# Attention scores in bundles of four and three beside a feed-forward product, and four parts instead of six behind the last value product

## The chip, the cores and the metric

The kernel runs on one core of one Trainium2 chip. The metric is the device time of one execution in microseconds (us), as the median of several runs. A profiled execution is recorded beside them; its span runs from the first to the last instruction of the core, and its own device time is a little longer than its span.

## The reference

The program is attention without a softmax, followed by a normalised two-layer feed-forward block with a residual:

```
S, D = 448, 64                      # 8 batches, 12 heads
scores = q @ k.T / sqrt(D)
attn   = max(scores, 0) ** 2 / S
x      = (attn @ v)                 # heads side by side: (8, 448, 768)
xn     = (x - mean) / sqrt(var + 1e-6) * g_ln
out    = x + max(xn @ w_ch1, 0) @ w_ch2     # 768 -> 3072 -> 768
```

Inputs and output are float32; the kernel computes the products in bf16.

## The kernel before

The eight batches are worked on two at a time, as four pairs 0 to 3. A pair goes through attention, the first feed-forward product (768 to 3072, with ReLU) and the second one (3072 to 768, with the residual). The change lies in the stage that is run three times, once for each of the pairs 0, 1 and 2 in the loop `for pair in range(pairs - 1)`: there the second feed-forward product of one pair is interleaved on TensorE with the attention of the next. I call these stages 0, 1 and 2. Between them lie the stages of the first product (`ffn1_pair`, line 960 in the profile), which uses seven block products in place of eight (Strassen), with sums made on VectorE and GpSimd or fetched.

The interleaving is written out in program order, and each engine runs its instructions in that order (the kernel opens a manual schedule). Two lists are merged by `spread`:

- The main list holds the second product in **parts** (also called units). A part is three matmuls, 128 by 128 weights with 384 columns, so `K2 // PARTS * DH` = 1152 columns. Eight parts make one output tile, behind which VectorE adds the residual and SP stores it. In stages 0 and 1 these are lines 789 and 800; in stage 2 the second product is the Strassen form (lines 1136, 1175, 1193). Stage 0 has 96 parts, stage 1 has 76 and stage 2 has 92 in the main list.
- The side list holds attention. Six **groups** of four heads each (two batches, three groups a batch) have seven **slots** each: a slot is 64 keys against 448 queries for the four heads. I write s0 to s6 for a group's slots and P for its value product.

A slot (`scores`) is four matmuls of 64 by 64 by 448 on the four quadrants of TensorE (line 400) into one PSUM buffer `sc_ps`; ScalarE then applies ReLU out of PSUM into an `attn_sb` tile in SBUF (line 411); the tile is then squared, either by ScalarE (line 413, when `act` is set) or by VectorE (line 380, when `square_fresh` or `pending` comes by). The value product P (`values`) is 28 matmuls of 64 by 64 by 448, in seven steps of four (line 432), into a buffer `av_ps` of the same pool; VectorE scales it into `xT_sb` (line 438). The pool `ps_sc` has **three** buffers, handed out in turn, for slots, value products and the `mean_ps` of `fold_mean` (line 512) alike; the parts' accumulators come from another pool, of two buffers. A group's value product comes in the bundle in which the next group's scores begin.

Before, `attention` cuts the 42 slots into 14 bundles of three, whatever group they belong to, and puts P behind the first or second slot of a bundle, where that slot is number 1 or 2 of the next group. Three orders of a bundle result: three slots; slot, slot, P, slot; and slot, P, slot, slot. The last P stands alone. `spread` gives all 15 pieces the same share of the stage's columns (`period`). The third slot of a bundle is squared on ScalarE in stages 0 and 2, and in every third bundle in stage 1.

In front of the last P the hook "odd" puts one or two sums for the next stage on VectorE (lines 989 and 994). Behind the last P, the hook "start" puts two more there (`x_sum`, lines 905 and 906, read by the third and fifth product of the next stage), then come the last `few` = 6 parts, and then `stage["run"]` begins the next first product with PSUM buffers `m_ps` in the room that `ps_sc` had. In stage 0, `fold_beside` also hangs `fold_mean` (four short matmuls, a copy by ScalarE) and `fold_into` (VectorE, line 519) on numbered parts; `fold_mean` takes a `ps_sc` buffer.

Of the kernel before, what the change touches and what calls it, by code (L numbers as in the profile page):

```python
# [24 lines left out]
            done += 1  # L25


def spread(main, cost, side, costs, pending):

    period = (cost * len(main) + sum(costs)) / sum(c > 0 for c in costs)
    at, due, done, n, ago = 0, period - costs[0], 0, 0, 0
    for unit in main:
        unit()
        at += cost
        ago += 1
        if ago % 2:
            pending(1)
        if n < len(side) and at >= (due if costs[n] else done + 3 * cost):  # L40
            if costs[n]:
                pending()
            side[n]()
            if costs[n]:
                at += costs[n]
                due += period
                done = at
                ago = 0
            n += 1
    for unit in side[n:]:  # L50
        pending()
        unit()
    pending()
# [3 lines left out]
def kernel(  # L57
# [28 lines left out]
    B, H, S, D = q.shape  # L86
# [3 lines left out]
    J = S // HP  # L90
# [4 lines left out]
    K2 = d_ff // P  # L95
    S2 = 2 * S
    NT = S2 // P
    DH = d_model // 2
# [117 lines left out]
    for queue, name, lo, hi in ((nc.sync, "q", 0, FEW), (nc.scalar, "k", 0, FEW),  # L216
                                (nc.sync, "k", FEW, J), (nc.scalar, "q", FEW, J)):
        s = slice(lo * D, hi * D)
# [304 lines left out]
    def fold_beside(units):  # L523

        more = {4: [lambda: statistics(0, 0), lambda: roots(0, 0, 1)], 24: [lambda: odd_x_out(0, nc.sync)]}
        for o in range(0, K2, K1):
            more[30 + 2 * o] = [lambda o=o: odd_h_out(0, nc.sync, (o, o + K1))]
        for i, n in ((2, 0), (3, 2), (4, 26), (5, 47)):
            more.setdefault(n, []).append(lambda i=i: fold_mean(i))
        for o in range(4 * K1):  # L530
            more.setdefault(6 + o * 84 // 24, []).append(lambda o=o: fold_into(2 + o // K1, o % K1))

        def both(n, unit):
            unit()
            for f in more.get(n, ()):
                f()
        return [lambda n=n, unit=unit: both(n, unit) for n, unit in enumerate(units)]

    by_dma = 2
# [96 lines left out]
    def attention(bs, hooks):  # L636

        lo, hi = bs[0] * G, (bs[-1] + 1) * G
        seq = [(n, i) for n in range(lo, hi) for i in range(J)]

        def item(n, i, act):
            scores(n, (i,), FULL, act)
            ahead = 3 if n + 3 < LATE else 2
            if i == J - 1 and n + ahead < len(groups) and (ahead == 3 or n + 2 >= LATE) and n != LATE - 1:
                transposed(n + ahead)  # L650

        def product(n):
            values(n, FULL)
            if n + 4 <= LATE:
                load(n + 4, "v")
            elif n + 3 > LATE:
                if n == LATE - 1:
                    put_off.append((n + 3, "v"))
                else:
                    load(n + 3, "v")  # L660

        squares = {by_dma: (0, 1, 2), by_dma + 2: (0,), B - 2: (0, 1, 2)}.get(bs[0], ())

        def bundle(items, at, turn):
            for o, it in enumerate(items):
                item(*it, o == 2 and turn in squares)
                if o == at:
                    product(it[0] - 1)
        units, costs, due = [], [], [[]]
        for s in range(0, len(seq), 3):  # L670
            items = seq[s:s + 3]
            at = max((o for o, (n, i) in enumerate(items[:2]) if n > lo and i in (1, 2)), default=-1)
            units.append(lambda items=items, at=at, s=s: bundle(items, at, s // 3 % 3))
            n = items[at][0] - 1
            costs.append((len(items) + (J if at >= 0 else 0)) * S)
            due.append([hooks[n - lo]] if at >= 0 and n - lo in hooks else [])
            for f in due.pop(0):
                units.append(f)
                costs.append(0)
        units.append(lambda: product(hi - 1))  # L680
        costs.append(J * S)
        return units, costs, due[0]


    xtok, rstd, moments = {}, {}, {}
# [1 line left out]
    def tokens_part(pair, lo, hi, chunks):  # L687

        for c in chunks:
            nc.sync.dma_start_transpose(xt_room[:, c, lo:hi], xT[pair][:, c, lo * P:hi * P])  # L690
# [89 lines left out]
    PARTS = 8  # L780
# [531 lines left out]
    units, side = ffn1_units(0, BLK[0][0]), attention_block(0, BLK[0][1])  # L1312
    units, late = units[:-4], units[-4:]
# [13 lines left out]
    units = ffn1_units(0, BLK[0][1])  # L1327
# [10 lines left out]
    side = {}  # L1338
# [61 lines left out]
    for pair in range(pairs - 1):  # L1400
        last = pair == pairs - 2
        following = {}

        def hook(name):
            if not following:
                following.update(ffn1_pair(
                    pair + 1, keep=pair == 0, given=pair > 0, late=last,
                    between=(between_one, between_two, between_three)[pair]))
                if pair:
                    tokens_room(pair + 1)  # L1410
            following[name]()
            if (pair, name) in soon:
                tokens_part(pair + 1, *soon[pair, name])
        if last:
            mm = [ps_mm.tile([P, 512], fp32, tag="mm", name="o_ps") for _ in range(2)]
            zs = [x_room.rearrange("p b c s -> p (b c s)")[:, 3 * KH * P:3 * KH * P + 2 * DH].bitcast(fp32),
                  room0[:, 9:].rearrange("p c n -> p (c n)").bitcast(fp32)]
            h_sum_tiles()
            head, units, _ = strassen_units(pair, mm, lambda t: mm[::-1] if t % 2 else mm)
        else:  # L1420
            units = ffn2_units(pair)
            head, units = (units[:PARTS // 2], units[PARTS // 2:]) if pair else ([], units)
        if pair:
            for unit in head:
                unit()
            stage["close"]()
            if pair == 1:
                odd_h_out(pair, nc.sync, (8, KH), (8 + KH, K2))
            narrow.close()
            ps_sc = open_wide()  # L1430
        else:
            units = fold_beside(units)
        if pair == 1:
            w2_sum_tiles()
            units = beside_of(units, dict(zip((20, 36, 50), w2_sum_units("t6"))))
        beside, costs, left = attention(
            [2 * pair + 2, 2 * pair + 3], {G - 1: lambda: hook("even"), 2 * G - 2: lambda: hook("odd")})
        few = 3 * PARTS // 4
        spread(units[:-few], K2 // PARTS * DH, beside, costs, square_fresh)
        for f in left:  # L1440
            f()
        wide.close()
        hook("start")
        ps_m = open_narrow()
        for unit in units[-few:]:
            unit()
        store_now()
        stage = following
        if pair == 0:
# [49 lines left out]
```

## Time and profile before

Three runs took 512.58, 512.78 and 513.10 us. The profiled execution took 512.57 us.

| | us |
|---|---|
| median of the runs | 512.78 |
| profiled execution | 512.57 |
| its span | 510.6 |
| stage 0, attention beside the second product (99.70 to 166.94 of the span) | 67.2 |
| stage 1 (213.70 to 274.07; it begins with the end of a first product) | 60.4 |
| stage 2 (320.70 to 390.48; likewise) | 69.8 |
| the two first products between them (166.94 to 213.70, 274.07 to 320.70) | 46.8 and 46.6 |
| from 390.48 to the end | 120.1 |

A line of the timeline gives the start in us, the duration in us, the engine, the line of the kernel, the operation with output and input tiles, the count, and in brackets the idle time ahead of it and who ended it. Neighbouring instructions of one kind are merged into one line. The ends of matmuls are modelled, so that one line overlaps the start of the next; a stretch of TensorE is better read from start to start.

### The profile page before, as it was taken

The page shows a single profiled execution, that of the slowest core. Times are in us where ns is not written, and L with a number is a line of the kernel's source. Part 1 is how long each engine was busy: PE and PEld are TensorE (multiplying, and loading weights), DVE is VectorE, ACT ScalarE, POOL GpSimd, SP SyncE. Part 2 cuts the span into 40 slices and gives each one's busy share as a digit, 9 for nine tenths or more (in the row PEclk, how much of TensorE's full clock was granted, in tenths as well). Part 3 has the DMA queues.
Part 4 walks back from the last instruction along what each step waited for, and adds up shares of the span by engine and source line. Part 5 has one row for each costly group of instructions (what it writes and reads, how often), then busy time and mean ns, then how long its engine had stood idle before and what let it go on. Part 6 is the DMA issues. An engine that isn't in the chain of part 4 may idle for free.

```text
span 510.6 us, 11501 instructions
## 1 busy us (share of the span) xinstructions
PE 503.1 (99%) x4545; PEld 297.9 (58%) x4545; DVE 388.2 (76%) x747; ACT 315.3 (62%) x519; POOL 130.0 (25%) x180
## 2 busy tenths in 40 slices
PE   8999999999999999999999999999999999999996
PEld 6677778955555555555555555555555555566663
DVE  4875755697998988768878888578869688677663
ACT  5966776578887566667883666489884677300000
POOL 8335102011412486002111995011000231000000
PEclk9999999999999999999999999999999999999999
DMA  9999999999999975739993878349936943622222
GB/s 198 206 206 206 211 206 143 135 195 177 203 203 223 219 228 152 191 87 163 269 170 75 177 167 140 61 78 179 194 69 164 224 131 94 230 64 63 63 62 62
DMA packets 136743, 80.25 MB, mean 157 GB/s; under 512 B 92418, under 2 KB 132610, under 8 KB 136690
## 3 DMA queue, kind: packets, MB, share of 16 engines
q1 hardware_dynamic: 106402, 46.59, 43.9%
q0 software_dynamic: 28272, 29.92, 36.7%
q10 hardware_dynamic: 2016, 3.02, 2.4%
q8 instruction: 35, 0.57, 0.5%
q14 instruction: 18, 0.15, 0.1%
HBM read 66.65 MB, written 19.86 MB: 169 GB/s over the span
## 4 chain that ended last, share of the span: by engine, by line
PE 92%; DMA 5%; POOL 1%; ACT 1%; DVE 1%; issue 1%; DVEq 0%; ACTq 0%; POOLq 0%
PE m_ps L960 28%; PE o_ps L789 17%; PE m_ps L1175 11%; PE o_ps L1175 11%; PE h_ps L728 7%; PE sc_ps L400 7%; PE av_ps L432 6%; DMA w<-in_moe_w_ch_dram 3%; PE h_ps L773 2%; DMA v_sb<-in_v_dram 2%; PE o_ps L1136 2%; PE h_ps L755 1%; ACT attn_sb L411 1%; PE tr_ps L278 1%; PE sum_ps L465 0%
## 5 line engine op out<-in xcount | busy, mean ns | idle before, releaser
L411 ACT ACTIVATE attn_sb<-sc_ps 128x896 bf16<-128x896 f32 (+4 forms) x150 | 126.2, 902 | 27.1 <-PE sc_ps L400 20.8
L964 ACT ACTIVATE hT_sb<-m_ps 128x448 bf16<-128x448 f32 x144 | 78.2, 543 | 51.8 <-PE m_ps L960 49.1
L789 PE MATMUL o_ps<-w,hT_sb 128*128 128x384 bf16 x528 | 92.2, 327 | 0.0
L789 PEld LDWEIGHTS <-hT_sb 128*128 128x128 bf16 x528 | 49.0, 98 | 39.8 <-issue 10.1
L380 DVE TENSOR_TENSOR attn_sb<-attn_sb 128x896 bf16<-128x896 bf16 x93 | 55.6, 617 | 8.0 <-ACT attn_sb L411 8.0
L728 PE MATMUL h_ps<-x_room,w 128*128 128x192 bf16 (+2 forms) x384 | 44.0, 263 | 0.2 <-DMA w<-in_moe_w_ch_dram 0.2
L438 DVE TENSOR_SCALAR xT_sb<-av_ps 128x896 bf16<-128x896 f32 (+2 forms) x30 | 27.1, 903 | 22.3 <-PE av_ps L432 22.2
L1175 PEld LDWEIGHTS <-hT_sb 128*128 128x128 bf16 x312 | 30.0, 98 | 21.6 <-issue 2.1
L1175 PEld LDWEIGHTS <-x_room 128*128 128x128 bf16 x288 | 27.5, 98 | 20.2 <-issue 2.5
L728 PEld LDWEIGHTS <-w 128*128 128x128 bf16 x384 | 33.8, 97 | 7.2 <-issue 1.8
L960 PEld LDWEIGHTS <-w 128*128 128x128 bf16 x246 | 24.0, 97 | 22.7
L1042 DVE TENSOR_TENSOR m_ps<-x_room,m_ps 128x448 f32<-128x448 f32 x36 | 22.6, 628 | 18.4 <-ACT hT_sb L964 18.2
L413 ACT ACTIVATE attn_sb<-attn_sb 128x896 bf16<-128x896 bf16 x33 | 31.4, 950 | 1.0
L960 PEld LDWEIGHTS <-w_sum 128*128 128x128 bf16 x210 | 20.5, 98 | 19.3 <-DVE w_sum L936 0.4
L705 DVE BATCH_NORM_STATS2 stats<-xtok_sb 128x6 f32<-128x384 bf16 x56 | 28.3, 547 | 3.1 <-DMA xtok_sb<-xT_sb 3.1
L187 POOL DMA_DIRECT2D k_sb<-in_k_dram x15 | 10.7, 711 | 78.2 <-DMA kT_sb<-k_sb 51.3
L187 POOL DMA_DIRECT2D v_sb<-in_v_dram x20 | 14.2, 715 | 61.1 <-PE sc_ps L400 52.4
L519 DVE SCALAR_TENSOR_TENSOR w<-w,g_sb,x_room 128x512 bf16<-128x512 bf16 x36 | 27.3, 787 | 3.0 <-ACT x_room L515 3.0
L960 PE MATMUL m_ps<-x_sum,w 128*128 128x448 bf16 x120 | 29.1, 352 | 0.0
L1024 ACT COPY x_room<-m_ps 128x448 f32<-128x448 f32 x36 | 19.1, 532 | 15.4 <-PE m_ps L960 14.4
L400 PE MATMUL sc_ps<-qT_sb,kT_sb 64*64 64x448 bf16 x392 | 27.9, 358 | 0.0
L432 PE MATMUL av_ps<-attn_sb,v_sb 64*64 64x448 bf16 (+2 forms) x532 | 26.9, 331 | 0.4 <-DVE attn_sb L380 0.4
(202 smaller groups left out, 895.5 us busy)
## 6 DMA issues: line engine op xcount, KB each, us to landing
out_dram<-o_room SPq DMA_DIRECT2D x108, 96.0 KB, 2.4
w<-in_moe_w_ch_dram POOLq DMA_DIRECT2D x12, 384.0 KB, 14.3
w<-in_moe_w_ch_dram POOLq DMA_DIRECT2D x4, 1152.0 KB, 20.1
q_sb<-in_q_dram POOLq DMA_DIRECT2D x20, 224.0 KB, 5.7
v_sb<-in_v_dram POOLq DMA_DIRECT2D x20, 224.0 KB, 5.8
k_sb<-in_k_dram POOLq DMA_DIRECT2D x15, 224.0 KB, 5.3
kept<-room SPq DMA_DIRECT2D x4, 480.0 KB, 3.2
kept<-w_sum SPq DMA_DIRECT2D x16, 96.0 KB, 2.4
```

The lines of the kernel that those rows point to most:

```text
L380: nc.vector.tensor_mul(a, a, a)
L400: nc.tensor.matmul(ps[cols, r, o * w:(o + 1) * w], g["k"](i)[rows, cols], g["q"](i, r)[rows, blk[0]:sum(blk), cols], start=True, stop=True)
L411: nc.scalar.activation(a, ps[:, :, :len(slots) * w], ACTF.Relu)
L413: nc.scalar.activation(a, a, ACTF.Square)
L432: nc.tensor.matmul(ps[cols, hh, :w], v_sb[rows, pr, j * D:(j + 1) * D], g["attn"][i][rows, r, :], start=(j == 0), stop=(j == J - 1))
L519: nc.vector.scalar_tensor_tensor(w, w, g_sb[:, c:c + 1], fold["means"][i % 2].rearrange("p (h n) -> p h n", h=2), op0=ALU.mult, op1=ALU.add)
L705: nc.vector.bn_stats(stats[:, n], xtok[pair][:, n * G:(n + 1) * G, t, :])
L728: nc.tensor.matmul(ps[:, :w + more], w1[:, c, ni * P:(ni + 1) * P], xc[b][:, c, s.start:s.stop + more], start=(c == 0), stop=(c == K1 - 1))
L789: nc.tensor.matmul(ps[:, :DH], hT[pair][:, ki, t * P:(t + 1) * P], w2[:, ki, cols], start=(o == 0), stop=(o == K2 - 1))
L960: nc.tensor.matmul(ps, *at, start=(first and c == 0), stop=(c == KQ - 1), skip_group_check=not first)
L964: nc.scalar.activation(hT[pair][:, n + KH * row, half * S:(half + 1) * S], ps, ACTF.Relu)
L1175: nc.tensor.matmul(ps, x[:, ki], y[ki] if isinstance(y, list) else y[:, ki], start=(first and ki == 0), stop=(ki == KH - 1), skip_group_ch ...
```

## The change

`spread` takes the number of slots of each piece. It sets the first piece behind two parts, gives every piece a share of the stage in proportion to its slots, and keeps the last P for behind the loop. `attention` cuts by group: the first group into slots 3, 2 and 2; every other group into a bundle of four, in the order s0 s1 P s2 s3 (P of the group before), and a bundle of three. That makes 13 bundles and the last P, in place of 14 and the last P. ScalarE squares s3 of each group, and in stages 0 and 2 s6 too. `few` goes from 6 parts to 4. Two `fold_mean` calls move by five parts back and one part ahead.

```diff
-def spread(main, cost, side, costs, pending):
-    period = (cost * len(main) + sum(costs)) / sum(c > 0 for c in costs)
-    at, due, done, n, ago = 0, period - costs[0], 0, 0, 0
+def spread(main, cost, side, costs, slots, pending):
+    free = 2 * cost
+    total, ahead = cost * len(main) + sum(costs) - free - costs[-1], sum(slots)
+    at, due, done, n, ago = 0, free, 0, 0, 0
...
-        if n < len(side) and at >= (due if costs[n] else done + 3 * cost):
+        if n < len(side) - 1 and at >= (due if costs[n] else done + 3 * cost):
...
-                due += period
+                due += total * slots[n] / ahead
...
-        for i, n in ((2, 0), (3, 2), (4, 26), (5, 47)):
+        for i, n in ((2, 0), (3, 2), (4, 31), (5, 46)):
             more.setdefault(n, []).append(lambda i=i: fold_mean(i))
...
-        squares = {by_dma: (0, 1, 2), by_dma + 2: (0,), B - 2: (0, 1, 2)}.get(bs[0], ())
-
-        def bundle(items, at, turn):
+        squares = (3,) if bs[0] == by_dma + 2 else (3, J - 1)
+
+        def bundle(items, at):
             for o, it in enumerate(items):
-                item(*it, o == 2 and turn in squares)
+                item(*it, it[1] in squares)
                 if o == at:
                     product(it[0] - 1)
-        units, costs, due = [], [], [[]]
-        for s in range(0, len(seq), 3):
-            items = seq[s:s + 3]
-            at = max((o for o, (n, i) in enumerate(items[:2]) if n > lo and i in (1, 2)), default=-1)
...
+        units, costs, slots, due = [], [], [], [[]]
+        for n in range(lo, hi):
+            parts = (0, 4, J) if n > lo else (0, 3, 5, J)
+            for i, j in zip(parts, parts[1:]):
+                items, at = range(i, j), 1 if n > lo and i == 0 else -1
+                units.append(lambda items=[(n, i) for i in items], at=at: bundle(items, at))
+                costs.append((len(items) + (J if at >= 0 else 0)) * S)
+                slots.append(len(items))
...
-        few = 3 * PARTS // 4
-        spread(units[:-few], K2 // PARTS * DH, beside, costs, square_fresh)
+        few = PARTS // 2
+        spread(units[:-few], K2 // PARTS * DH, beside, costs, slots_of_each, square_fresh)
```

More of the change, by code (lines that the diff above doesn't have):

```diff
@@ L643, in attention @@
         lo, hi = bs[0] * G, (bs[-1] + 1) * G
-        seq = [(n, i) for n in range(lo, hi) for i in range(J)]
         def item(n, i, act):
@@ L660, in product @@
                     load(n + 3, "v")
-        squares = {by_dma: (0, 1, 2), by_dma + 2: (0,), B - 2: (0, 1, 2)}.get(bs[0], ())
-        def bundle(items, at, turn):
+        squares = (3,) if bs[0] == by_dma + 2 else (3, J - 1)
+        def bundle(items, at):
             for o, it in enumerate(items):
-                item(*it, o == 2 and turn in squares)
+                item(*it, it[1] in squares)
                 if o == at:
                     product(it[0] - 1)
-        units, costs, due = [], [], [[]]
-        for s in range(0, len(seq), 3):
-            items = seq[s:s + 3]
-            at = max((o for o, (n, i) in enumerate(items[:2]) if n > lo and i in (1, 2)), default=-1)
[L673 to L679, printed above, removed]
+        units, costs, slots, due = [], [], [], [[]]
[6 more added lines that the diff above has]
+                slots.append(len(items))
+                due.append([hooks[n - 1 - lo]] if at >= 0 and n - 1 - lo in hooks else [])
+                for f in due.pop(0):
+                    units.append(f)
+                    costs.append(0)
+                    slots.append(0)
         units.append(lambda: product(hi - 1))
         costs.append(J * S)
-        return units, costs, due[0]
+        return units, costs, slots, due[0]
     xtok, rstd, moments = {}, {}, {}
@@ L1435 @@
             units = beside_of(units, dict(zip((20, 36, 50), w2_sum_units("t6"))))
-        beside, costs, left = attention(
+        beside, costs, slots_of_each, left = attention(
             [2 * pair + 2, 2 * pair + 3], {G - 1: lambda: hook("even"), 2 * G - 2: lambda: hook("odd")})
-        few = 3 * PARTS // 4
-        spread(units[:-few], K2 // PARTS * DH, beside, costs, square_fresh)
+        few = PARTS // 2
+        spread(units[:-few], K2 // PARTS * DH, beside, costs, slots_of_each, square_fresh)
         for f in left:
```

## The prediction

> **What bounds the kernel.** First the head of the page: TensorE is busy for 503.1 of 510.6 us, and the clock granted to it is 1.00 in every stage, so whatever lengthens or shortens its stream shows in the end.
>
> ```profile
> span 510.6 us, 11501 instructions
> PE 503.1 (99%) x4545; PEld 297.9 (58%) x4545; DVE 388.2 (76%) x747; ACT 315.3 (62%) x519; POOL 130.0 (25%) x180
> ```
>
> Busy hides what TensorE loses inside, so next its timeline in stage 0, read from start to start. Here is a bundle "slot, P, two slots", parts, a bundle "two slots, P, slot", parts, and a bundle of three slots.
>
> ```profile
> 146.38 0.38 PE L400 MATMUL sc_ps<-spare 64*64 64x448 bf16 x4
> 146.59 1.49 PE L432 MATMUL av_ps<-attn_sb,v_sb 64*64 64x448 bf16 x28
> 147.91 0.62 PE L400 MATMUL sc_ps<-spare 64*64 64x448 bf16 x8
> 148.47 2.61 PE L789 MATMUL o_ps<-w,hT_sb 128*128 128x384 bf16 x15
> 151.01 0.57 PE L400 MATMUL sc_ps<-spare 64*64 64x448 bf16 x8
> 151.41 0.36 PE L400 MATMUL sc_ps<-qT_sb,kT_sb 64*64 64x448 bf16 x4
> 151.70 3.59 PE L789 MATMUL o_ps<-w,hT_sb 128*128 128x384 bf16 x21
> 155.22 0.57 PE L400 MATMUL sc_ps<-qT_sb,kT_sb 64*64 64x448 bf16 x8
> 155.62 1.49 PE L432 MATMUL av_ps<-attn_sb,v_sb 64*64 64x448 bf16 x28
> 156.94 0.36 PE L400 MATMUL sc_ps<-qT_sb,kT_sb 64*64 64x448 bf16 x4
> 157.24 2.12 PE L789 MATMUL o_ps<-w,hT_sb 128*128 128x384 bf16 x12
> ```
>
> P's seven steps take 156.94 - 155.62 = 1.32 us, 0.19 a step of four matmuls; a slot is one such step. 21 matmuls of the parts take 155.22 - 151.70 = 3.52 and 15 take 151.01 - 148.47 = 2.54, so one takes 0.163, a part 0.49, and 0.10 of a stretch is left for going over to the quadrants. Three slots take 0.69 against 3 x 0.19 = 0.57: 0.12 for coming back. One alternation costs about 0.22.
>
> Third, ScalarE's ReLUs of the same two bundles, each asked for alone.
>
> ```profile
> 147.18 0.92 ACT L411 ACTIVATE attn_sb<-sc_ps 128x896 bf16<-128x896 f32 x1 [0.88 <-PE av_ps L432]
> ...
> 155.65 0.92 ACT L411 ACTIVATE attn_sb<-sc_ps 128x896 bf16<-128x896 f32 x1 [0.69 <-PE sc_ps L400]
> ...
> 156.47 0.91 ACT L411 ACTIVATE attn_sb<-sc_ps 128x896 bf16<-128x896 f32 x1
> ```
>
> In the second bundle (start 155.22) the first ReLU runs from +0.43 to +1.35, the second from +1.25 to +2.16. A slot leaves TensorE every 0.19 us and ScalarE every 0.81. So long as three buffers are enough, that is hidden. The first bundle shows what it looks like when they are not: its last slot takes the buffer of its first, whose ReLU starts late, since its tile waits for P's first steps, and ends at 148.10. TensorE could begin that slot at 147.91 + 0.19 = 148.10; a last slot with the way back takes 0.30 (157.24 - 156.94), so it began at 148.47 - 0.30 = 148.17. A buffer is free 0.07 us after the end of its ReLU.
>
> **Bundles of four.** In s0 s1 P s2 s3, s2 takes the buffer of s0 and s3 that of s1, three requests back. TensorE would reach s2 at +1.72 and s3 at 1.72 + 0.19 = +1.91. The buffer of s0 is free at 1.35 + 0.07 = 1.42, in time. That of s1 is free at 2.16 + 0.07 = 2.23: TensorE waits 0.32 us, with the parts queued behind s3, and nothing fills that. All value products but the last of each stage stand in such bundles: 5 x 3 = 15, so **+4.8**. ScalarE reaches the bundle free: a bundle of three with one square occupies it until 0.43 + 2.54 + 0.95 = 3.92 behind its start, and the next starts after 0.69 + 7 x 0.49 = 4.1 (stages 0 and 2); in stage 1, 5 or 6 parts and no square of s6, 2.97 against at least 3.1. The bounds: 0.25, if the end of s1 comes without the latency, and 0.6, if a root (0.3) or copy delays s0; 3.8 to 9.0. I take 0.32, as six of the nine bundles "two slots, P, slot" have the second ReLU at +1.24 to +1.27.
>
> The Trainium skill, page "TensorEngine Tiling (Array Packing)", section "PSUM Bottleneck", speaks against this change: tiling speeds up TensorE but not the evacuation of PSUM, which may then be the bound. The trace agrees, 0.19 against 0.81; the rule gives no other number.
>
> **What goes.** The six bundles "slot, P, two slots" lose their 0.07: **-0.4**. Each stage has 14 pieces in place of 15, one alternation less: 3 x 0.22 = **-0.65**, between -0.3 (only one of the two crossings) and -1.0. By the Trainium skill, "TensorEngine Tiling (Array Packing)", section "Key Properties", a change of tiling mode drains TensorE; the Trainium skill's "TensorE: Matmul & The Clock Gate", section "Single matmul latency", has 398 cycles beside the columns at 2.4 GHz, 0.17 us a crossing, an estimate of 0.33 an alternation. By it this term would be -1.0; the rows decide for -0.65.
>
> **The last P.** Working out `spread` for both versions, the last bundle and the last P have 7 parts between them in stages 0 and 2 (5 before) and 5 in stage 1 (4 before). The rows of the last P in stages 1 and 2:
>
> ```profile
> 268.96 1.32 PE L432 MATMUL av_ps<-attn_sb,v_sb 64*64 64x448 bf16 x21
> 270.64 0.57 PE L432 MATMUL av_ps<-attn_sb,v_sb 64*64 64x448 bf16 x7 [0.36 <-DVE attn_sb L380]
> 271.14 3.10 PE L789 MATMUL o_ps<-w,hT_sb 128*128 128x384 bf16 x18
> ...
> 385.73 1.88 PE L432 MATMUL av_ps<-attn_sb,v_sb 64*64 64x448 bf16 x28
> 387.54 1.15 PE L1175 MATMUL o_ps<-w,hT_sb 128*128 128x384 bf16 x6
> ```
>
> Alone, P takes 1.49 (162.52 to 164.01 in stage 0). Stage 1 took 2.18, stage 2 1.81: 0.69 and 0.32 lost to the square of s6, which the sixth step needs. Two more parts (0.98) cover stage 2; one more (0.49) leaves 0.2 to 0.3 in stage 1. **-0.7**, between -1.0 and 0.
>
> **Four parts behind it.** The next stage begins 0.98 us sooner behind P. Its second product needs `xT_sb` and the third the first `x_sum`; VectorE has these 1.2 and 2.1 us behind P (164.01: 165.21, 166.16), TensorE wants them at 1.95 + 0.57 = 2.5 and 3.1. That cover holds. What is late next is VectorE's list behind them: in stage 0 the weight sum of line 936 for the first product's second round. Now it ends at 171.00, and 0.14 is lost (its eighth product is wanted at 166.94 + 7 x 0.57 = 170.92 and begins at 171.06). Half of its chain waited for TensorE; from `x_sum` on (166.93) it needs about 3.5 us, so 170.4, and TensorE wants it at 169.95: 0.5, **+0.4** net. In stage 1 `x_sum` ends 2.9 behind P, two roots and a residual come to 4.0, lines 1026 and 1028, the next `x_sum` and line 1042 take 0.6 to 0.85 each, so 6.7; the ninth product wants line 1042 at 1.95 + 8 x 0.57 = 6.5: **+0.25**. In stage 2 the sums of the hook "odd" are done earlier beside P: 0. If all the cover were missed it would be 3 x 0.98 = 2.9; at least 0.
>
> **The rest.** The first bundle of stage 0 now stands between two `fold_mean` calls; the second takes the buffer of the stage's first slot: that ReLU ends near 102.3, TensorE is there at 102.1: **+0.2** (0 to 0.5). ScalarE squares 30 tiles in place of 33, VectorE three more of 0.62: hidden, for both have gaps in these stages (53 and 57 us busy of 67 in stage 0); without cover 1.9. DMAs, with POOL's and SP's queues, keep their order (key and query transposes at s6, value loads behind P), and s6 of the first group comes 7 parts sooner, so nothing is later: 0. The moved `fold_mean` calls keep two parts to the next bundle, more than the 0.58 of their copy: 0.
>
> **Sum.** 4.8 - 0.4 - 0.65 - 0.7 + 0.4 + 0.25 + 0.2 = +3.9. Against the profiled execution, 512.57 + 3.9 = **516.5 us** (span 514.5). The median of the runs is 0.2 above that execution, within what separates the runs.
>
> **Rivals.**
> - *The wait at s3 isn't there.* Then 512.57 - 0.9 = 511.7, faster. It decides if the buffer of s1 is free before +1.91. For it: TensorE shows no idle time before line 400 in these stages so far, and no slot has yet been asked for so soon behind P. Against: the 0.07 above counts from the record's end, and all six such bundles show the same 0.55 from second slot to part. 9%.
> - *The wait is there, and the gains are larger* (alternations by the crossing of 0.33, both waits of the last P gone, no loss at the stage starts): 512.57 + 4.8 - 0.4 - 1.0 - 1.0 = 515.0; with the lower bound 0.25 for s3, 514.0. 10%.
> - *The cover of six parts was needed.* VectorE falls behind and each next stage starts late by the full 0.98: 2.9 in place of 0.65, 516.5 + 2.3 = 518.8. For it: VectorE is without a gap from 164.12 to 167.86 in stage 0. Against: the first three products have 0.6 to 1.3 us of slack. 8%.
> - *The bundles even out and the wait is partly earned back*, in stalls within stages that the rows don't name (stage 2 has about 0.5 us unexplained): half of 4.8 lost, 512.57 + 2.4 - 0.9 - 0.5 = 513.6, within the noise of no change. 5%.
>
> The forecast holds 68%. About 0.2% (1.0 us) is what a measurement of this kernel tells from no change. Slower by more: forecast, larger gains and lost cover, 86%; within: 5%; faster: 9% (the first rival ends on that bound). The range 514.0 to 518.6 leaves out the first and the last rival and the far end of the lost cover; its lower end is the lower bound of s3 with all gains, its upper one takes 0.45 a bundle.
>
> **What would show it.** In TensorE's timeline each bundle of four would have P and s2 1.3 apart and s3 begin 0.5 behind s2 in place of 0.19, with an idle time that ScalarE's line 411 ended: 15 times. From the bundle's start to the next part 2.5 us in place of 2.2. The last P takes 1.49 in stages 0 and 2. The first row of line 960 behind stage 0 begins 1.95 behind P, and its eighth product shows a wait for line 936. I am wrong if s3 begins within 0.25 of s2, or if ScalarE starts s0 later than +0.5.

## The result and the profile after

The kernel after takes **518.31 us** (median of six runs, 517.47 to 519.72); the kernel before took 513.03 beside it. The ratio is 1.0108, with a 95% interval of 1.0091 to 1.0125: 5.3 us slower. Forecast were 516.5 with a range of 514.0 to 518.6.

The head of the profile after (its profiled execution took 519.72 us, 7.1 more than that of before):

```profile
span 517.6 us, 11508 instructions
PE 505.3 (98%) x4545; PEld 299.2 (58%) x4545; DVE 390.0 (75%) x750; ACT 312.6 (60%) x516; POOL 130.4 (25%) x180
```

Of the 7.0 us by which the span has grown, only 2.2 are busy time of TensorE, for the same 4545 instructions. TensorE's timeline in stage 0: a bundle of four, parts, a bundle of three, parts, the last P, and the start of the next first product.

```profile
156.48 0.57 PE L402 MATMUL sc_ps<-qT_sb,kT_sb 64*64 64x448 bf16 x8
156.89 1.49 PE L434 MATMUL av_ps<-attn_sb,v_sb 64*64 64x448 bf16 x28
158.21 0.87 PE L402 MATMUL sc_ps<-qT_sb,kT_sb 64*64 64x448 bf16 x8
159.01 3.59 PE L792 MATMUL o_ps<-w,hT_sb 128*128 128x384 bf16 x21
162.53 0.76 PE L402 MATMUL sc_ps<-qT_sb,kT_sb 64*64 64x448 bf16 x12
163.22 3.59 PE L792 MATMUL o_ps<-w,hT_sb 128*128 128x384 bf16 x21
166.74 1.52 PE L434 MATMUL av_ps<-attn_sb,spare 64*64 64x448 bf16 x28
168.19 2.12 PE L792 MATMUL o_ps<-w,hT_sb 128*128 128x384 bf16 x12
170.15 1.30 PE L963 MATMUL m_ps<-xT_sb,room 128*128 128x448 bf16 x6
```

s0, s1 and P run as before. Then s2 and s3 take 159.01 - 158.21 = 0.80 us; two slots ahead of parts take 0.49 elsewhere. That is the wait at s3, 0.31, and the merged row hides it: there is no bracket, because the idle time is inside the row. The wait has to be read from start to start. From the bundle's start to the next part it is 2.53.

ScalarE's row for the same bundle, four ReLUs in one line:

```profile
156.92 3.43 ACT L413 ACTIVATE attn_sb<-sc_ps 128x896 bf16<-128x896 f32 x4 [0.69 <-PE sc_ps L402]
```

It begins at +0.44, and a ReLU leaves every 0.84. The second ends at about +2.16, so s1's buffer comes free some 0.3 later than TensorE wants it.

The table holds, for every kernel that ran, TensorE's time of each stretch from start to start (stages 0, 1, 2 and the first product behind each). "Ahead" is the time before stage 0, which the change doesn't touch. It varied from 99.55 to 101.30 from one profile to the next, so single profiles are compared by the stages. From the last of these stretches to the end of the span it was 73.6 to 73.8 in all.

| kernel | ahead | 0 | first | 1 | first | 2 | first | span | median |
|---|---|---|---|---|---|---|---|---|---|
| before | 99.70 | 67.24 | 46.77 | 60.36 | 46.67 | 69.74 | 46.53 | 510.6 | 512.78 |
| after | 100.84 | 69.31 | 47.16 | 61.11 | 47.08 | 71.76 | 46.72 | 517.6 | 518.31 |
| P behind s0 | 99.55 | 72.62 | 47.17 | 65.44 | 47.29 | 74.70 | 46.72 | 527.1 | 529.58 |
| six parts behind | 99.75 | 69.56 | 46.77 | 61.80 | 46.66 | 72.57 | 46.53 | 517.2 | 519.14 |
| before, four parts behind | 99.65 | 67.27 | 47.15 | 60.10 | 47.31 | 69.52 | 47.11 | 511.7 | 513.84 |
| s1 by VectorE | 100.53 | 73.15 | 47.17 | 61.32 | 47.30 | 70.45 | 46.72 | 520.2 | 520.03 |
| two repairs | 99.94 | 68.68 | 47.16 | 61.11 | 47.29 | 71.86 | 46.72 | 516.6 | 518.80 |
| three, two, two | 100.03 | 69.87 | 47.16 | 62.36 | 47.08 | 74.01 | 46.54 | 520.6 | 522.64 |
| loads later | 101.30 | 69.46 | 47.17 | 61.11 | 47.09 | 70.61 | 46.72 | 517.0 | 518.64 |
| half from PSUM | 99.65 | 68.03 | 47.16 | 59.91 | 47.10 | 69.60 | 46.72 | 511.8 | 514.54 |
| both places | 100.05 | 68.71 | 47.17 | 61.10 | 47.09 | 70.60 | 46.72 | 515.0 | 517.39 |
| pair moved | 99.60 | 69.42 | 47.90 | 61.10 | 47.31 | 71.71 | 46.78 | 517.4 | 519.20 |
| before, last P | 99.59 | 67.25 | 46.77 | 59.94 | 46.68 | 69.38 | 46.76 | 510.0 | 512.35 |

After less before, over the six stretches: 2.07 + 0.39 + 0.75 + 0.41 + 2.02 + 0.19 = **5.83** us. Of the profiled execution's 7.1, another 1.14 lie ahead of stage 0. The medians differ by 5.3: the profiled execution is the longest of the six, so what follows is the account of that one.

Going through these stretches row by row, three losses appear that the forecast had at nothing. The first two, in stage 0:

```profile
134.80 0.57 PE L402 MATMUL sc_ps<-qT_sb,kT_sb 64*64 64x448 bf16 x8
135.62 1.52 PE L434 MATMUL av_ps<-attn_sb,v_sb 64*64 64x448 bf16 x28 [0.25 <-ACT x_room L517]
136.94 0.69 PE L402 MATMUL sc_ps<-qT_sb,kT_sb 64*64 64x448 bf16 x8
...
145.69 0.92 PE L434 MATMUL av_ps<-attn_sb,v_sb 64*64 64x448 bf16 x13
147.01 0.95 PE L434 MATMUL av_ps<-attn_sb,v_sb 64*64 64x448 bf16 x15 [0.40 <-DVE attn_sb L382]
147.61 0.72 PE L402 MATMUL sc_ps<-spare 64*64 64x448 bf16 x8
```

P begins 0.82 behind its bundle in place of 0.40: 0.42 lost to the copy of `mean_ps`, whose buffer it takes. The next P is split: 147.61 - 145.69 = 1.92 in place of 1.32, 0.60 lost to squares. VectorE and POOL at that place:

```profile
141.03 3.01 DVE L382 TENSOR_TENSOR attn_sb<-attn_sb 128x896 bf16<-128x896 bf16 x2
```
```profile
141.22 0.93 POOL L924 TENSOR_TENSOR room<-w 128x384 bf16<-128x384 bf16 x1
142.10 0.91 POOL L929 TENSOR_TENSOR room<-w 128x384 bf16<-128x384 bf16 x1
```

Two squares take 3.01 in place of 1.15, the first of them 2.47; it ends 0.49 behind POOL's two weight sums. The third loss is in stage 2:

```profile
358.21 0.76 PE L402 MATMUL sc_ps<-qT_sb,kT_sb 64*64 64x448 bf16 x12
360.07 3.57 PE L1178 MATMUL o_ps<-w,hT_sb 128*128 128x384 bf16 x21 [1.10 <-DVE o_room L1196]
```
```profile
359.40 0.62 DVE L1196 SCALAR_TENSOR_TENSOR o_room<-o_ps,rstd_sb,xtok_sb 128x384 f32<-128x384 f32 x1 [3.66 <-DMA out_dram<-o_room]
```

The stretch takes 1.86 in place of 0.69: VectorE stood 3.66 us before an output buffer whose store had not landed, and TensorE 1.17 behind it. In the window from 345 to 361 us the eight stores took 5.9 us from issue to landing (second row), against 2.2 over the whole page (first row); the 224 KB loads of keys, queries and values ran beside them. The kernel before has the same loads in that window, and its six stores there took 5.0, but it wants no output buffer at that moment: its next output comes at 361.76, 12.3 behind the last one; here it is wanted at 355.74, 3.7 behind.

```profile
out_dram<-o_room SPq DMA_DIRECT2D x108, 96.0 KB, 2.2
```
```profile
out_dram<-o_room SPq DMA_DIRECT2D x8, 96.0 KB, 5.9
v_sb<-in_v_dram POOLq DMA_DIRECT2D x2, 224.0 KB, 6.6
k_sb<-in_k_dram POOLq DMA_DIRECT2D x1, 224.0 KB, 5.2
q_sb<-in_q_dram POOLq DMA_DIRECT2D x1, 224.0 KB, 6.7
```

### The profile page after: what moved, and what is told of

Its sections match the earlier page's. It is cut to its first block, busy times and chain, and to the rows that moved or that the text cites. A ratio compares the mean times of both kernels' runs of the same rounds, so it can differ in the third digit from the quotient of the medians.

```text
span 517.6 us, 11508 instructions
## 1 busy us (share of the span) xinstructions
PE 505.3 (98%) x4545; PEld 299.2 (58%) x4545; DVE 390.0 (75%) x750; ACT 312.6 (60%) x516; POOL 130.4 (25%) x180
## 4 chain that ended last, share of the span: by engine, by line
PE 61%; DVE 3%; ACT 2%; issue 1%; DMA 1%; SPq 1%; DVEq 0%; ACTq 0%
PE m_ps L963 27%; PE m_ps L1178 11%; PE o_ps L792 9%; PE o_ps L1178 8%; PE sc_ps L402 3%; ACT attn_sb L413 2%; PE o_ps L1139 2%; PE av_ps L434 1%; DMA out_dram<-o_room 1%; DVE attn_sb L382 1%; DVE x_sum L908 0%; DVE xT_sb L440 0%; DVE w L521 0%; DVE x_sum L909 0%; SPq L349 0%
## 5 line engine op out<-in xcount | busy, mean ns | idle before, releaser
L382 DVE TENSOR_TENSOR attn_sb<-attn_sb 128x896 bf16<-128x896 bf16 x96 | 59.5, 636 | 9.8 <-ACT attn_sb L413 9.6
L415 ACT ACTIVATE attn_sb<-attn_sb 128x896 bf16<-128x896 bf16 x30 | 28.5, 950 | 1.0
L521 DVE SCALAR_TENSOR_TENSOR w<-w,g_sb,x_room 128x512 bf16<-128x512 bf16 x36 | 25.8, 741 | 3.0 <-ACT x_room L517 3.0
```

The costliest lines, as they stand in the source:

```text
L382: nc.vector.tensor_mul(a, a, a)
L415: nc.scalar.activation(a, a, ACTF.Square)
```

## The experiments

**P behind s0.** The kernel after with P one slot sooner: three slots then follow the request of P's buffer.

```diff
-                items, at = range(i, j), 1 if n > lo and i == 0 else -1
+                items, at = range(i, j), 0 if n > lo and i == 0 else -1
```

> The changed kernel with P behind s0 in place of s1: s0 P s1 s2 s3. Theory: s3 now takes the buffer of P, which VectorE empties only 1.1 us after starting 0.22 behind P's end, so until about +2.9, and TensorE wants it at +1.91: a wait of 1.0 in place of 0.32, 15 times, +10 us: 528.5 (525 to 531). Rival (the number of slots in a bundle or the squares cost, not the buffers): the same four slots and the same squares, no change, 518.3.

529.58 us (529.28 to 533.0), ratio 1.0326 (1.0266 to 1.0386). Now the wait is long enough to have a row of its own:

```profile
158.03 1.49 PE L434 MATMUL av_ps<-attn_sb,v_sb 64*64 64x448 bf16 x28
159.35 0.55 PE L402 MATMUL sc_ps<-qT_sb,kT_sb 64*64 64x448 bf16 x8
160.72 0.38 PE L402 MATMUL sc_ps<-qT_sb,kT_sb 64*64 64x448 bf16 x4 [0.82 <-DVE xT_sb L440]
```

s3 takes the buffer of P itself, which VectorE has yet to scale. s3 begins 1.37 behind s1 in place of 0.38, 0.99 lost. The rule "three requests back" holds, and it gives the size of the wait as well as its place.

**Six parts behind.** The kernel after with the old `few`.

```diff
-        few = PARTS // 2
+        few = 3 * PARTS // 4
```

> The changed kernel with six parts behind the last value product in place of four, as before. Theory: the starts of the three next stages lose 0.99 us in the changed kernel's profile (0.39, 0.41, 0.19) against 0.14 with six, so 0.85 less: 517.5. Rival (the cover of two parts is worth its whole 0.98 in each stage): 2.9 less, 515.4. If the shifted places of the bundles matter more than the cover, either sign.

519.14 us (518.86 to 519.55), ratio 1.0101 (1.0061 to 1.0141). The three first products are back at 46.77, 46.66 and 46.53, so the four parts do cost 0.99. But `spread` then has two parts fewer to lay out, and every bundle shifts: a P loses 0.9 to a `mean_ps` copy in stage 0 and one 0.4 to squares in stage 1, whose last P loses 0.7 again, and two copies of line 1203 cost 2.0 in stage 2. The time was expected 0.8 lower and came 0.8 higher: nothing is gained, and the count can't be separated from the places it moves.

**Before, four parts behind.** The same line alone, the other way round, in the kernel before.

> The kernel before with four parts behind the last value product as the only edit. Theory: +0.85 at the starts of the next stages, about -0.45 at the last value product of stage 1, which gets one part more: +0.4 against before, 513.4. Rival (the cover is worth its whole length): +2.9, 515.9.

513.84 us (513.39 to 515.18), ratio 1.0005 (0.998 to 1.003). The first products take 0.38, 0.64 and 0.58 longer, 1.60 in all where 0.85 was expected; stages 1 and 2 gain 0.26 and 0.22. In the trace the span is 1.1 longer; the medians can't tell it from nothing.

**s1 by VectorE.** The kernel after, the ReLU of s1 in the bundles of four on VectorE, so that two engines empty PSUM.

```diff
-        nc.scalar.activation(a, ps[:, :, :len(slots) * w], ACTF.Relu)
+        s = ps[:, :, :len(slots) * w]
+        if dve:
+            nc.vector.tensor_scalar_max(a, s, 0.0)
+        else:
+            nc.scalar.activation(a, s, ACTF.Relu)
```

> The changed kernel with one edit: in the bundles of four, VectorE applies the ReLU of s1 out of PSUM (ScalarE did); its square stays on VectorE. Theory (s3 waits for ScalarE's ReLU of s1, 0.31 us in 15 bundles): VectorE begins s1 near +0.64 of the bundle, ends by about +1.75, and TensorE wants the buffer at +1.91, so s3 begins 0.19 behind s2 where VectorE was free at +0.64; 3 to 4.5 us less than the changed kernel's 518.3: 514 to 515.5. Where VectorE is busy with a square or a residual of 0.6 the wait stays, so that the gain may be half. Rival (the bundles of four cost by the load on the engines): VectorE gets 15 x 1.1 us more, ScalarE 15 x 0.8 less, and the time stays within 1 us of 518.3 or goes up.

520.03 us (519.45 to 522.16), ratio 1.0140 (1.0119 to 1.0162). TensorE's waits:

```profile
PE sc_ps L402 <- DVE attn_sb L415: 4.7, 8, 1.9
```

In five of the 15 bundles the wait is gone, and in two it is under 0.2; in the other eight TensorE waits for VectorE, 4.7 us in total and up to 1.9, as VectorE has other work in hand when s1 comes. Stage 0 loses 3.8, but 1.7 of that isn't a wait: behind the longest one TensorE's granted clock is 0.50 for 3.4 us, and 24 matmuls of parts take 5.68 from start to start in place of 4.00 (the profiled execution, 522.16, is the longest of the four).

```profile
150.13 0.38 PE L402 MATMUL sc_ps<-spare 64*64 64x448 bf16 x4 [1.93 <-DVE attn_sb L415]
150.44 5.75 PE L796 MATMUL o_ps<-w,hT_sb 128*128 128x384 bf16 x24
```

Stage 2 gains 1.3, of which 1.2 is the wait for the output buffer, which isn't there in this run. An engine with a quarter of its time free is not free at the moment when it is asked.

**Two repairs.** The kernel after, `fold_mean(5)` three parts later, and the second half of stage 2's stores on POOL's queue.

```diff
-        for i, n in ((2, 0), (3, 2), (4, 31), (5, 46)):
+        for i, n in ((2, 0), (3, 2), (4, 31), (5, 49)):
...
-(nc.sync, nc.scalar if last else nc.sync)
+(nc.sync, nc.scalar if last else nc.gpsimd if pair == B // 2 - 2 else nc.sync)
```

> The changed kernel with two edits in different stages, read apart by the trace. Stage 0: the last fold_mean behind part 49 in place of 46, so behind the bundle that it stood just ahead of. Stage 2: the second half of each output tile is stored from POOL's queue in place of SP's. Theory for stage 0: P2 no longer waits for the copy of mean_ps (0.44 in the changed kernel's trace), its s3 then waits the usual 0.31 in place of 0.13: 0.25 less. Theory for stage 2: VectorE's wait of 3.7 us for an output buffer comes from stores queued on SP behind the key and query transposes, so the wait goes, with the 1.2 us that TensorE lost there. Together 1.4 less: 516.9. Rival for stage 2: the stores wait for the DMA engines themselves, or POOL's queue stands behind its own loads: the wait of VectorE stays.

518.80 us (518.19 to 519.74), ratio 1.0110 (1.0095 to 1.0126). The first repair holds: each of the five bundles of four in stage 0 loses 0.31, and no P waits for the copy. Stage 0 is 0.63 shorter in place of 0.25, since the 0.60 lost to squares isn't there either. The second fails, and the time as a whole isn't below that of the kernel after:

```profile
DVE o_room L1196 <- DMA out_dram<-o_room: 6.0, 2, 3.8
```

The stores on POOL's queue took 5.4 to land and those on SP's 4.2, so moving them to another queue doesn't help.

**Loads later.** The kernel after; in stage 2 the key and query loads of the next group but one are asked for at s5 of the next group in place of s6 of this one, so that they don't run beside those stores.

```diff
-            load(n + 2, "kq")
+            put_late.append((n + 2, "kq"))
...
+            if i == 5 and put_late:
+                load(*put_late.pop(0))
```

> The changed kernel with the key and query loads of stage 2 issued at s5 of the next group in place of straight behind the key and query transposes at s6. Theory: VectorE's wait of 3.7 us for an output buffer near 356 comes from the stores of the output landing 5.9 us after their issue (2.2 over the whole kernel) because loads of 224 KB, released by the same transposes, share the DMA engines with them; the wait shrinks to under 1, and TensorE's 1.2 us at 359 goes: 517.1. Rival (the stores are late because SP stands at the transposes until s6 of that group has run): the wait stays, 518.3.

518.64 us (517.61 to 520.0), ratio 1.0106 (1.0072 to 1.0139). Stage 2 takes 70.61 in place of 71.76, and no row of TensorE waits for line 1196 (here 1198). The two stores that VectorE waited for, in the kernel after (issued at 352.82 and 353.41) and here (353.44 and 354.03):

```profile
out_dram<-o_room SPq DMA_DIRECT2D x2, 96.0 KB, 5.3
```
```profile
out_dram<-o_room SPq DMA_DIRECT2D x2, 96.0 KB, 2.2
```

In the kernel after, the first two of the loads were asked for at 352.33 and 353.04, here the first at 355.02, behind these two stores. Over the whole window the median is still 5.5, for the later stores now run beside the loads, but no output waits for those. The rival is half true: in both kernels the first of the two was issued 5.1 behind its sum, as SP's queue stood at the transposes. The total doesn't show the gain: the time ahead of stage 0 was the longest of all profiles, 101.30, and stage 0's losses grew by 0.15.

**Three, two, two.** The kernel after, every group cut into 3, 2 and 2, so that P stands in a bundle of three.

```diff
-            parts = (0, 4, J) if n > lo else (0, 3, 5, J)
+            parts = (0, 3, 5, J)
```

In the last group of stage 2 two slots read the next sum (line 997) in place of the query tile, and wait 2.3 us for it; so that stage isn't read.

> The changed kernel with every group cut into bundles of 3, 2 and 2 slots (s0 s1 P s2, s3 s4, s5 s6), as it has for its first group. No slot asks for a buffer that ScalarE still holds, and every engine does the same work. Theory: the 15 waits at s3 go (13 of 0.31, two shorter: -4.4) and five alternations a stage are added (15 x 0.22 = +3.3): 1.1 less than the changed kernel, 517.2, and no idle time of TensorE ahead of a slot in the trace. Rival (the waits are not what the bundles of four cost): only the alternations, 518.3 + 3.3 = 521.6.

522.64 us (521.41 to 522.77), ratio 1.0175 (1.0137 to 1.0212). By its total this lies 5.4 above the theory and near the rival, so the total doesn't speak for the theory; the rows have to. Not one wait at s3 is left, and five alternations a stage are added, but a P in stage 0 loses 1.3 to squares (0.6 in the kernel after) and one in stage 1 0.8, and stage 2 has the wait just named. Less the named losses (P's waits for squares above all), stage 0 is 67.97 against 66.82 in the kernel after, stage 1 60.47 against 59.33: 1.15 and 1.14 for five, **0.23 an alternation**. The forecast had 0.22 from rows; the estimate by the Trainium skill's "TensorE: Matmul & The Clock Gate", section "Single matmul latency", was 0.33, and the measurement decides against it.

**Half from PSUM.** The kernel after; ScalarE frees s1's buffer after half its elements.

```diff
...
+        if half:
+            nc.scalar.activation(a[:, 0], s[:, 0], ACTF.Relu)
+            nc.scalar.activation(a[:, 1], a[:, 0], ACTF.Relu)
...
```

> The kernel after, in which ScalarE takes only the first half of s1's scores out of PSUM in the bundles of four, and fills the second half of its tile from the first half in SBUF (so the second half of these scores is replaced by the first in what is computed). ScalarE has about as much to do as before (two instructions in place of one), but the PSUM buffer of s1 should be free about 0.4 us sooner: 1.25 + 0.5 + 0.07 = +1.8 behind the bundle's start, where TensorE wants it at +1.91. Theory (the wait at s3 is for the ReLU of s1 and nothing else): no wait at s3 in the 15 bundles, P, s2 and s3 close up, s2 to the next part 0.49 in place of 0.80, so 13 to 15 x 0.31 = 4.0 to 4.7 us less, 513.6 to 514.3 with what the long squares and the output buffer still cost. Rival (the time is lost to something that goes with four slots and a value product in one bundle, say the load on ScalarE or VectorE, and moves elsewhere): 517 to 518.5. If the two halves take longer than estimated, the waits are shorter but there: 515 to 517.

514.54 us (513.57 to 515.74), ratio 1.0033 (1.0022 to 1.0043): 3.8 us less than the kernel after, by the medians of two comparisons, and 0.2 short of what the theory gave. ScalarE and TensorE in a bundle of four:

```profile
122.76 0.92 ACT L418 ACTIVATE attn_sb<-sc_ps 128x896 bf16<-128x896 f32 x1 [0.44 <-PE sc_ps L402]
123.57 0.54 ACT L415 ACTIVATE attn_sb<-sc_ps 128x448 bf16<-128x448 f32 x1
124.14 0.58 ACT L416 ACTIVATE attn_sb<-attn_sb 128x448 bf16<-128x448 bf16 x1
```
```profile
122.72 1.49 PE L439 MATMUL av_ps<-attn_sb,spare 64*64 64x448 bf16 x28
124.05 0.55 PE L402 MATMUL sc_ps<-qT_sb,kT_sb 64*64 64x448 bf16 x8
124.53 1.64 PE L797 MATMUL o_ps<-w,hT_sb 128*128 128x384 bf16 x9
```

The buffer is given back at 124.11, and s2 and s3 take 0.48. No wait at s3 is left in 12 of the 15 bundles, 0.1 to 0.17 in three, with ScalarE's work larger than before (1.05 for the tile of s1 in place of 0.84). So the wait is for the release of this one buffer, and not for ScalarE's load. Against this bundle without a wait (2.21 from its start to the next part) the 2.53 of the kernel after is 0.32 more. The six stretches are 4.6 shorter than in the kernel after: 3.9 are these waits, 0.6 the output buffer's (0.61 is left of 1.17), 0.6 the squares' (the long instruction has hit a `fold_into`), less 0.5 for a longer wait for `mean_ps`.

**Both places.** The kernel after with the repair of `fold_mean(5)` and the later loads together.

> The kernel after with both repairs of places that the prediction costed at nothing: fold_mean(5) behind part 49 in place of 46, and the key and query loads of stage 2 asked for at s5 of the next group in place of s6 of this one. Theory (what is left beyond the kernel before is the 15 waits of 0.31, the stage starts of 1.0, less the alternations and the last P): stage 0 68.7, stage 2 70.6 of TensorE's time from start to start, where the kernel after has 69.3 and 71.8, and a time of 516.5 to 517.0. Rival (long squares beside POOL's sums come by themselves, wherever the calls stand): stage 0 69.3 or longer, 517.3 to 518.3.

517.39 us (517.08 to 518.57), ratio 1.0090 (1.0075 to 1.0105). Stages 0 and 2 take 68.71 and 70.60 as expected. VectorE's long instruction is there, but has hit a `fold_into`, for which no P waits. The time is 0.4 above what was expected, and by the medians only 0.9 of the 1.75 that the six stretches gained is there. The six stretches are now 4.08 above those of before, where the forecast's sum was 3.9; the medians of this comparison differ by 4.6.

**Pair moved.** It was to put POOL's pair of sums at 141 us on VectorE.

```diff
-                sums_early(1)
+                sums_early(1, nc.vector)
```

> The kernel after, in which the pair of weight sums that the hook of stage 0 puts on POOL (lines 924 and 929, 0.93 and 0.91 us) is put on VectorE instead. In the kernel after, one VectorE square took 2.47 us in place of 0.62 while POOL worked on that pair, and P of the third group lost 0.6 waiting for squares. Theory (VectorE's instruction is held by POOL's pair, whichever instruction it hits): no VectorE instruction of stage 0 between 136 and 146 takes over 1.1 us, two sums of about 0.35 appear on VectorE, P is not split by a wait for line 382 and stage 0 takes 68.7 in place of 69.3. Rival (the long instruction comes from something else at that place, such as the DMA traffic of the loads): it is still there, and stage 0 takes 69.3 or more. The time as a whole changes by no more than 0.6 us, 517.6 to 518.4.

519.20 us (517.85 to 519.24), ratio 1.0101 (1.0043 to 1.0159). The edit missed its object: the pair at 141 is another round's and stayed on POOL, the long square with it. What moved is a set behind the last P, 0.36 + 0.29 + 0.22 on VectorE, and it shows something else:

```profile
172.23 0.73 PE L963 MATMUL m_ps<-x_sum,w 128*128 128x448 bf16 x3 [0.77 <-DVE x_room L1029]
```

0.87 more in VectorE's list behind P cost the next first product 0.74 (47.90 in place of 47.16). Behind the last P of stage 0 VectorE has next to no slack left.

**Before, last P.** The kernel before; ScalarE squares the third slot of the last bundle in stage 1 too, and in stage 2 one part more lies ahead of the last P.

```diff
-bundle(items, at, s // 3 % 3)
+bundle(items, at, 0 if s == len(seq) - 3 else s // 3 % 3)
...
-        few = 3 * PARTS // 4
+        few = 3 * PARTS // 4 - last
```

> The kernel before with its last value products covered by other means: the last slot of stage 1 is squared by ScalarE, and in stage 2 five parts stay behind the last P in place of six. Theory (from the profile of before): P of stage 1 loses 0.75 to VectorE's square of s6, ScalarE has it 0.6 earlier; P of stage 2 loses 0.38, one part more ahead of it covers that; nothing else moves, so 0.9 less than before, 512.1. Rival: what is saved at P is lost in the next stage, whose VectorE list sets its start: no change, 513.0.

512.35 us, ratio 0.9966 (0.9933 to 1.0000). Stages 1 and 2 are 0.42 and 0.36 shorter, a first product 0.23 longer. It was run again:

> The kernel before with the two edits at the last value products, once more, to narrow the interval: theory 0.6 to 0.9 us less than before, 512.2 to 512.4; rival no change.

512.46, ratio 0.9987 (0.9969 to 1.0006), the stages equal to within 0.01 us. About half a microsecond is there in both traces; the medians alone leave it between 0.7% and nothing. It is the only kernel here with a median below that of before.

## Why the prediction was right in its direction and 1.8 us short

The terms against the profile after:

| term | forecast | measured |
|---|---|---|
| 15 waits at s3 | +4.8 | +4.28 |
| "slot, P, two slots" and alternations | -0.4, -0.65 | -1.0 together |
| last P | -0.7 | -0.87 |
| starts behind four parts (stages 0, 1, 2) | +0.4, +0.25, 0 | +0.39, +0.41, +0.19 |
| `fold_mean` at the first bundle | +0.2 | +0.22 |
| the rest | 0 | +2.19 |
| sum | +3.9 | +5.8 |

- **The waits at s3** are confirmed by three experiments: with P one place sooner they grow to 0.99; with the buffer freed sooner, or with P in a bundle of three, they go. Of the 15, 12 are 0.31; the first of stage 1 is 0.26, and two of stage 0 are 0.13 and 0.17 since TensorE was late there already. The total time bears this out in the first two; in the third only the rows do.
- **Alternations.** The 1.0 is what the other terms leave of the sum. The rows bear both terms out: the six bundles "slot, P, two slots" took 2.09 from start to next part against 2.02 for the others with P, 0.4 in all, and "three, two, two" gives 0.23 an alternation, 0.69 for three.
- **Last P.** It takes 1.45, 1.70 and 1.45 us to the next part, where it took 1.48, 2.18 and 1.81. The 0.25 left in stage 1 is the forecast's 0.2 to 0.3.
- **Four parts behind it.** The size is near (0.99 for 0.65), the place is not. The forecast looked for the loss at line 936 (here 939) in stage 0, before the eighth product, and at line 1042 (here 1045) in stage 1, before the ninth. From start to start, TensorE loses 0.20, 0.44 and 0.19 in the three stages before the fifth product, which goes on in a PSUM buffer that VectorE's first sum, line 1029 (1026 before), has to read first; the eighth product of stage 0 loses 0.34 in place of 0.14, and nothing is lost at line 1045.

```profile
174.66 0.74 PE L963 MATMUL m_ps<-x_sum,w_sum 128*128 128x448 bf16 x3 [0.17 <-DVE w_sum L939]
...
281.13 0.73 PE L963 MATMUL m_ps<-x_sum,w 128*128 128x448 bf16 x3 [0.28 <-DVE x_room L1029]
```

  So the +0.4 of stage 0 came true by half through its own mechanism and by half by luck, and the step that failed is "That cover holds", which looked at `xT_sb` and the first `x_sum` but not at line 1026 behind them. "Before, four parts behind" has the same loss before the fifth product in all three stages (0.19, 0.44, 0.59), and "pair moved" lengthens it. In stage 2 it is 0.19 in the kernel after in place of that 0.59, which fits the forecast's argument that the sums of the hook "odd" are done earlier; they don't take it to 0.
- **"The rest" is the step that failed.** Three sentences of it. "The moved `fold_mean` calls keep two parts to the next bundle, more than the 0.58 of their copy: 0" counted the copy's duration, not when it may begin: it waited for VectorE's `fold_into`, which reads the room it writes.

```profile
134.98 0.59 ACT L517 COPY x_room<-mean_ps 128x512 f32<-128x512 f32 x1 [1.15 <-DVE w L521]
```

  The copy ended at 135.57 and P began at 135.62, cost 0.42; "two repairs" took it away by three parts more. "VectorE three more of 0.62: hidden, for both have gaps in these stages" looked at busy time; a P needs its squares at one moment, and a single held instruction there cost 0.60. "DMAs, with POOL's and SP's queues, keep their order", with "so nothing is later: 0", took order for time. The order is kept, and stores ran beside loads before too; but with the outputs at other moments VectorE wanted the first of its three output buffers back at 355.74, while the stores from it, held on SP's queue until 352.82 and 353.41, were still landing beside the loads: 1.17 of TensorE's time. "Loads later" removed it, and 1.15 with it. All three cost time that the forecast had at 0; that 518.31 still lies 0.3 inside the range is luck, since the range's upper end allowed for a dearer wait at s3 (0.45 a bundle) and not for these.
- Repairing the first and third place ("both places") leaves 4.08 against 3.9 in the traces (4.6 by the medians). The forecast's sum is right within that for what it named, though at the starts by partly other waits. It also means that the repairs don't rescue the change: the waits cost 4.28, and alternations, bundles and last P less the later starts bring 1.0 + 0.87 - 0.99 = 0.88.
- **The rivals.** "The wait isn't there" and "evens out" fell. "Gains are larger" needed 0.33 an alternation; it is 0.23. "Cover of six needed" came out near the right time, 518.8, but by the wrong mechanism: the starts cost 0.99 in all, not 2.9.

## What to carry to other kernels

With n buffers in a pool and a slow reader, write down for each request which request it follows by n places and when that one's reader ends; the wait it gives was right to 0.01 us here (0.32 forecast, 0.31 to 0.32 measured), and splitting that one reader removed it. An edit that reorders work beside a saturated engine also moves what other engines and queues do at each moment: "same order" and "busy share has room" aren't reasons for a zero, so look up what each consumer finds at its own moment, and keep some microseconds for it. Short waits hide inside merged rows of the timeline; read such an engine from start to start.

## What was not expected of the hardware

- A VectorE instruction with two inputs in SBUF beside POOL's pair of sums is held until the pair ends. In 12 of the 14 profiles, those of the kernels before and after among them, one such instruction ended 0.49 to 0.56 us behind POOL's second sum: six times a square of 0.62, which took 1.69 to 2.63, and six times a `fold_into` of 0.73, which took 1.60 to 2.32. In the kernel before it was a `fold_into`, and no P waited for it. Its row and POOL's in the kernel before:

```profile
136.84 2.32 DVE L519 SCALAR_TENSOR_TENSOR w<-w,g_sb,x_room 128x512 bf16<-128x512 bf16 x1
```
```profile
137.69 0.91 POOL L926 TENSOR_TENSOR room<-w 128x384 bf16<-128x384 bf16 x1
```

  In "two repairs" it went the other way: VectorE was busy without a gap, and POOL's sums took 2.11 and 1.35.

```profile
144.18 2.11 POOL L924 TENSOR_TENSOR room<-w 128x384 bf16<-128x384 bf16 x1
146.26 1.35 POOL L929 TENSOR_TENSOR room<-w 128x384 bf16<-128x384 bf16 x1
```

  The Trainium skill, "SBUF — State Buffer", section "Who interferes with whom", has this: a VectorE instruction with two SBUF inputs contends with a GpSimd instruction that reads SBUF, and the one that comes second blocks. The trace agrees that the two hold each other up; by the recorded starts it doesn't show that the second is the one held, as VectorE's square begins 0.19 ahead of POOL's first sum in the kernel after. No run took POOL's pair away, as the one that should have moved another pair, so the cause rests on the coincidence in 12 profiles and on two contrasts: in "P behind s0" VectorE had no such instruction in hand until 0.17 before the pair's end, and none was held; and 16 sums of line 1029 in the kernel after, with one input in PSUM, overlap POOL's sums in the first products, and none took over 0.62.
- A store of 96 KB that lands in 2.2 us took 5.9 beside loads of 224 KB, on SP's queue, and 5.4 on POOL's; the same two stores took 5.3 with the loads asked for beside them, and 2.2 with the loads behind them.
- A long wait of TensorE can cost more than itself. Behind the wait of 1.93 in "s1 by VectorE" and behind that of 2.27 in stage 2 of "three, two, two" the granted clock was 0.50 for 3.4 us; a matmul of the parts then took 0.32 in place of 0.163. Behind the shorter waits in the stages, up to 1.37, it was 1.00. Two cases don't show where the bound lies.
